# A decode step on one core: where three PV blocks stand among a softmax's steps, which engine takes a root, and how a mean is summed

## The chip, the cores and the metric

The kernel runs on one core of a Trainium2 chip. The metric is the device time of one execution in microseconds (us). Engines are called as the profile calls them: PE is TensorE's matmul and PEld its weight load, DVE is VectorE, ACT is ScalarE, POOL is GpSimd, and SP is SyncE, which here only issues transfers. All engines run their own instruction lists in order and wait for each other through semaphores.

## The reference

One token for each of 8 sequences goes through an attention block and a two-layer MLP block, each behind a layer norm. Only the last 2048 of the 8192 cached positions count.

```python
def _A_ref(x, k_cache, v_cache, wq, wo):          # x is layernormed: [8, 1, 512]
    # Hq = 32 query heads, Hkv = 8 cached heads, Dh = 128, W = 2048
    q = heads(x @ wq)
    k = jnp.repeat(k_cache[:, :, Sk - W:, :], 4, axis=1)
    v = jnp.repeat(v_cache[:, :, Sk - W:, :], 4, axis=1)
    p = _softmax(jnp.einsum("bhqd,bhkd->bhqk", q, k) * (Dh ** -0.5))
    o = jnp.einsum("bhqk,bhkd->bhqd", p, v)
    return o.reshape(B, Sq, Hq * Dh) @ wo

def _B_ref(x, w1, w2, w3, w4):                    # x is layernormed again
    ...                                           # the branch through w1, w2 shifts tokens
    x1 = x + hs                                   # with one token, hs is zero
    return x1 + _gelu(_layernorm(x1) @ w3) @ w4

h  = x + _A_ref(_layernorm(x), ...)
h2 = h + _B_ref(_layernorm(h), ...)               # the output, [8, 1, 512]
```

The second half needs two inverse roots of the variance of h. `r2` scales the first MLP product; `r1` scales the normed h that is added to the output.

## The kernel before, in words

**Items.** The work is cut into 64 items, one for each row (sequence) b and cached head g, numbered i = 8 b + g. An item has a K tile and a V tile of 2048 x 128. K is loaded four items at a time, V one at a time, all from SP's queue in the order in which the program issues them. V has 12 buffers: the load of V for item i waits until PE has used item i - 12 (`load_v`, L407).

**One loop over p.** The whole attention is written out by `for p in range(NITEM + LV + 1)` (L456), and each engine's order is the order of this loop. In step p PE transposes K of item p (L274), ACT and DVE copy the halves out (`evict`, L282 and L284), and PE does the scores of item p - 2 (`pe_QK`, L296). When a row's eight items are scored, its softmax is spread over the following steps: the maximum on DVE in step base = 8 b + 9 (`softmax_1`, L305); in base + 1 the maximum is turned by PE (L309) and joined and negated on DVE (`Mrow` L311, `negrow` L315); in base + 2 PE turns it back (L319), DVE copies it (`negcol`, L322), and ACT does the exponential (L323); in base + 3 PE transposes P (L333), DVE copies it out (`pT_sb`, L337) and prepares the sums (`lsel`, L341); in base + 4 PE adds them (L345) and DVE takes the reciprocal (`rL`, L347).

**PV in blocks of four.** For rows 0 to 6 the product with V is done for four items at once (`pe_PV4`, L365): 16 matmuls (L372) into the PSUM tile `o_rows`; ACT copies the result as bf16 (L379), DVE subtracts to get the rest that bf16 lost (L380). Some steps later `pe_oT` (L383) transposes both parts with 8 matmuls (L390), back into `o_rows`, and DVE scales the outcome into `oT_all` (L397). There is one `o_rows`: the next block waits for this scale. The last three such blocks begin at items 44 (row 5), 48 and 52 (row 6). Before the change they are issued like all others: block n in step n + 19, its transpose in step n + 20.

**The last row** goes item by item, from step 72 on: `pe_PV` with V as the stationary operand (L356), then its scale, and one step later its part of the output product. The first four heads go by `pe_wo_row` (L422), which also waits for the scale of block 52; the result is split in two bf16 parts (L429, L430), `pe_h0` adds them and x, and the other heads go by `pe_wo` (L449) into `hT_ps`, which then holds h transposed: 4 blocks of 128 features, 8 columns (sequences) each.

**The tail.** DVE copies h out (`hs`, L525), PE multiplies it with a matrix of ones to sum over the partitions (L527), DVE adds the four blocks (`msum`, L528) and subtracts the mean (`uT` L529 in bf16, `hc` L531). PE starts on w3 (L545), does the same sum for the squares in between (L550), and DVE reduces them to `vsum` (L554). POOL computes `r2` = (vsum + eps^2) to the power -0.5 in two instructions (L557, L558). DVE multiplies the product by it (`g_x`, L567, two halves), ACT applies Gelu (L569, two halves), and PE multiplies by w4 in three pieces as they land (L582). POOL goes on with `r1` (L570, L571), DVE makes `xb` (L572) and `fin` (L573) of it, adds the product (`fT`, L587), PE transposes it (L590), DVE copies it (L591), and SP stores it (L594).

Of the kernel before, what the change touches and what calls it, by code (L numbers as in the profile page):

```python
# [6 lines left out]
dt = mybir.dt  # L7
ACT = mybir.ActivationFunctionType
ALU = mybir.AluOpType
AX = mybir.AxisListType  # L10

B = 8
# [3 lines left out]
G = 8  # L16
# [8 lines left out]
EPS = 1e-5  # L25

NK = 3
KQ = 4
NV = 12
NKT = 4  # L30
LQK = 2
LV = 16
# [35 lines left out]
def bass_sequential_preLN__sliding_block_cached__mixer_s_mlp__decode_kernel(  # L68
# [19 lines left out]
    NITEM = NB * G  # L88
# [3 lines left out]
    with es:  # L92
        sb = lambda shape, dtype, name: es.enter_context(nc.sbuf_tensor(name, shape, dtype))
# [8 lines left out]
        ones_f = sb([128, 128], dt.float32, "ones_f")  # L102
# [7 lines left out]
        w4_sb = sb([128, FC, D], dt.bfloat16, "w4_sb")  # L110
        half = sb([128, B], dt.float32, "half")
        scratch = sb([128, 2], dt.float32, "scratch")

        x_sb = sb([B, D], dt.bfloat16, "x_sb")
        xln_b = sb([B, D], dt.bfloat16, "xln_b")
# [25 lines left out]
        orow = sb([128, 2, 512], dt.bfloat16, "orow")  # L141

        NH = KC * B
        hs = sb([128, NH], dt.float32, "hs")
        hc = sb([128, NH], dt.float32, "hc")
        hsq = sb([128, NH], dt.float32, "hsq")
        msum = sb([128, B], dt.float32, "msum")
        vsum = sb([128, B], dt.float32, "vsum")
        r1 = sb([128, B], dt.float32, "r1")
        r2 = sb([128, B], dt.float32, "r2")  # L150
        xb = sb([128, NH], dt.float32, "xb")
# [11 lines left out]
        sm = ps_t([128, 512], dt.float32, "sm")  # L163
# [4 lines left out]
        o_rows = ps_t([128, 512], dt.float32, "o_rows")  # L168
# [6 lines left out]
        PE, AC, DV, PO, SP = (Engine(S(n)) for n in ("s_pe", "s_act", "s_dve", "s_pool", "s_sp"))  # L175
# [7 lines left out]
        dma(AC, x_sb[:], A_x.rearrange("b s d -> (b s) d"), sem_x)  # L183
        X = (sem_x, 16)
        PO.op(lambda e: e.memset(half[:], -0.5))
        e_scr = PO.op(lambda e: e.memset(scratch[:], 1.0))
        e_xz = PO.op(lambda e: e.memset(xlnT[:], 0.0))
        e_iota = PO.op(lambda e: e.iota(iota_f[:], [[1, 128]], base=0, channel_multiplier=-1,
# [7 lines left out]
        e = DV.op(lambda e: e.bn_stats(st6[:, :], x_sb[:, :]), X)  # L196
        e = DV.op(lambda e: e.bn_aggr(mv[:, :], st6[:, :]), e)
        e = PO.op(lambda e: e.tensor_scalar(rstd[:, :], mv[:, 1:2], EPS, None, ALU.add), e)
        e = PO.op(lambda e: e.tensor_tensor(rstd[:, :], rstd[:, :], half[0:B, 0:1], ALU.pow), e)
# [7 lines left out]
        e = DV.op(lambda e: e.tensor_reduce(hsq[:, :], ident_f[:, :].rearrange("p (u h) -> p h u", u=4), AX.X, ALU.add))  # L207
# [9 lines left out]
        e = PE.op(pe_xT, e_xln, e_idb)  # L217
# [7 lines left out]
        for j in range(2):  # L225
# [9 lines left out]
            if j == 0:  # L235
                e = AC.op(lambda e: e.activation(qrow[:, 0, :], S_ps[0][:, :], ACT.Copy, scale=inv_sqrt_dh), e_q)  # L236
# [128 lines left out]
        def pe_PV4(i):  # L365
            b, g = divmod(i, G)
            v0 = i % NV

            def f(e):
                for c in range(NC):  # L370
                    u = c % 4
                    ins = e.matmul(o_rows[32 * u:32 * (u + 1), :], pT_sb[:, b % 2, c, :],  # L372
                                   vnat[:, v0:v0 + KQ, c * DH:(c + 1) * DH], start=(c < 4), stop=(c >= NC - 4),
                                   tile_position=(0, 32 * u), skip_group_check=True)
                return ins
            e_pv = PE.op(f, V(i), V(i + 1), V(i + 2), V(i + 3), e_pT[b], e_sc4.get(i - KQ))
            for k in range(KQ):
                e_PV[i + k] = e_pv
            e = AC.op(lambda e: e.activation(orow[:, 0, :], o_rows[:, :], ACT.Copy), e_pv, e_oT.get(i - KQ))  # L379
            e_olo[i] = DV.op(lambda e: e.tensor_tensor(orow[:, 1, :], o_rows[:, :], orow[:, 0, :], ALU.subtract), e)  # L380


        def pe_oT(i):  # L383
            b, g = divmod(i, G)

            def f(e):
                for t in range(KQ):
                    for part in range(2):
                        h = hq(g + t)
                        ins = e.matmul(o_rows[:, R * t:R * (t + 1)], orow[:, part, t * DH:(t + 1) * DH],  # L390
                                       sel32[:, h:h + R], start=(part == 0), stop=(part == 1), skip_group_check=True)
                return ins
            e_oT[i] = PE.op(f, e_olo[i], e_selb)
            e_scale[b] = e_sc4[i] = scale(b, slice(R * g, R * (g + KQ)), o_rows[:, 0:R * KQ], e_oT[i])

        def scale(b, heads, src, *waits):
            return DV.op(lambda e: e.tensor_tensor(oT_all[:, heads, b], src, rL[:, b % 2, heads], ALU.mult),  # L397
                         e_rL[b], e_oz, *waits)
# [13 lines left out]
        hT_ps = S_ps[0]  # L412
# [39 lines left out]
            e_wo.append(PE.op(f, e_sc7[g]))  # L452

        LAST = NB - 1
        E_LAST = G * LAST + G - 1 + LQK
        for p in range(NITEM + LV + 1):  # L456
            if p < NITEM:
                if p % KQ == 0:
                    load_k(p)
                if p == 1:  # L460
                    e_qblk = q_turn()
                pe_T(p)
                evict(p)
            if p in WO_AT:
                n = WO_AT.index(p)
                hh = H // len(WO_AT)
                dma(SP, wo_v[:, n * hh:(n + 1) * hh, :],
                    A_wo[n * hh * DH:(n + 1) * hh * DH, :].rearrange("(h p) n -> p h n", p=DH), sem_wo, e_q)
            for b in range(NB):
                base = G * b + (G - 1) + LQK  # L470
                if p == base + 1:
                    softmax_2(b)
                elif p == base + 2:
                    softmax_3(b)
                elif p == base + 3:
                    softmax_4(b)
                elif p == base + 4:
                    softmax_5(b)
            if 0 <= p - LQK < NITEM:
                pe_QK(p - LQK)  # L480
                b, g = divmod(p - LQK, G)
                if g == G - 1:
                    softmax_1(b)
            i = p - LV
            if 0 <= i < NITEM:
                load_v(i)
                b, g = divmod(i, G)
                heads = slice(R * g, R * (g + 1))
                if b < LAST:
                    if i % KQ == 0 and i:  # L490
                        pe_oT(i - KQ)
                    elif i % KQ == KQ - 1:
                        pe_PV4(i - KQ + 1)
                else:
                    if g == 0:
                        pe_oT(i - KQ)
                    dst = kbank[g % 3][:, 0:R]
                    pe_PV(i, dst, e_lo[NITEM - 1], e_hi[NITEM - 1], e_lo[NITEM - 2], e_hi[NITEM - 2],
                          e_sc7.get(g - 3))
                    e_sc7[g] = scale(b, heads, dst, e_PV[i])  # L500
            g = i - 1 - G * LAST
            if g == NR:
                pe_h0()
            if 0 <= g < NR:
                pe_wo_row(g)
            elif g >= NR:
                pe_wo(g)
# [9 lines left out]
        v3 = lambda t: t.rearrange("p (n b) -> p n b", b=B)  # L517
        vr = lambda t: t.rearrange("p (n b) -> p b n", b=B)

        def bc(t):  # L520
            a = t[:, :]
            return bass.AP(tensor=a.tensor, offset=a.offset, ap=[a.ap[0], [0, KC], [1, B]])


        e_hs = DV.op(lambda e: e.tensor_copy(hs[:, :], hT_ps[:, 0:NH]), e_wo[-1])  # L525
        st1, st2 = sm[:, 0:NH], o_rows[:, 0:NH]
        e = PE.op(lambda e: e.matmul(st1, ones_f[:, :], hs[:, :], start=True, stop=True), e_hs, e_rL[LAST])  # L527
        e_ms = DV.op(lambda e: e.tensor_reduce(msum[:, :], vr(st1), AX.X, ALU.add), e)  # L528
        e_u = DV.op(lambda e: e.scalar_tensor_tensor(v3(uT[:, :]), bc(msum), -1.0 / D, v3(hs[:, :]),  # L529
                                                     ALU.mult, ALU.add), e_ms)  # L530
        e_hc = DV.op(lambda e: e.scalar_tensor_tensor(v3(hc[:, :]), bc(msum), -1.0 / D, v3(hs[:, :]),  # L531
                                                      ALU.mult, ALU.add))
        e_sq = DV.op(lambda e: e.scalar_tensor_tensor(hsq[:, :], hc[:, :], (1.0 + EPS) / D, hc[:, :], ALU.mult, ALU.mult),
# [20 lines left out]
        e_vs = DV.op(lambda e: e.tensor_reduce(vsum[:, :], vr(st2), AX.X, ALU.add), e_st2)  # L554


        e = PO.op(lambda e: e.tensor_scalar(r2[:, :], vsum[:, :], EPS * EPS, None, ALU.add), e_vs)  # L557
        e_r2 = PO.op(lambda e: e.tensor_tensor(r2[:, :], r2[:, :], half[:, :], ALU.pow), e)  # L558

        def bcf(t):  # L560
            a = t[:, :]
# [3 lines left out]
        for n in range(2):  # L565
# [1 line left out]
            e = DV.op(lambda e, n=n, cs=cs: e.tensor_tensor(v3(g_x[:, cs]), v3(y_ps[n][:, 0:FH * B]), bcf(r2),  # L567
                                                            ALU.mult), e_y[n], e_r2)
            e_gT.append(AC.op(lambda e, cs=cs: e.activation(gT[:, cs], g_x[:, cs], ACT.Gelu_apprx_tanh), e))  # L569
        e = PO.op(lambda e: e.tensor_scalar(r1[:, :], vsum[:, :], EPS * (1.0 + EPS), None, ALU.add))  # L570
        e = PO.op(lambda e: e.tensor_tensor(r1[:, :], r1[:, :], half[:, :], ALU.pow), e)  # L571
        e = DV.op(lambda e: e.tensor_tensor(v3(xb[:, :]), v3(hc[:, :]), bc(r1), ALU.mult), e)  # L572
        e_fin = DV.op(lambda e: e.scalar_tensor_tensor(fin[:, :], xb[:, :], math.sqrt(1.0 + EPS), hs[:, :],  # L573
                                                       ALU.mult, ALU.add), e)

# [56 lines left out]
```

## Time and profile before

| | us |
|---|---|
| median of 3 runs (lowest, highest) | 201.53 (200.86, 202.16) |
| the profiled execution, its own time | 201.4 |
| its span | 199.2 |
| busy in that span: PE, PEld | 151.7, 99.7 |
| busy: ACT, DVE, POOL | 88.0, 83.1, 9.6 |
| transfers, from HBM | 79.18 MB, 398 GB/s over the span |

The span runs from the first to the last instruction of the profiled execution; the execution's time has 2.2 us more around it. All times in the lines below count from the start of the span. Transfers fill the 16 DMA engines for 96.8% of the span, but a share over the whole span hides that the last 6 us have none: what happens after the last K tile's landing is to be read from the chain of waits and the timeline of that stretch.

### The profile page before, as it was taken

To read this page: it belongs to the slowest core of one execution; us is meant where nothing else is said; L and a number is where in the kernel's file an instruction comes from. 1 tells how busy PE (TensorE), PEld (TensorE's weight loads), DVE (VectorE), ACT (ScalarE), POOL (GpSimd) and SP (SyncE) were. 2 spreads that over 40 slices of the span, in tenths; PEclk is the share of its full clock that TensorE was granted. 3 is DMA by queue.
4 is the path that set the end of the run, shared out by engine and by line. 5 is a ranking of instruction groups with operands and counts; after the bars stand their busy time and mean duration, and the time that the engine had idled before them with its cause. 6 is when DMAs were issued, how large, how long until landed. Compare 5 with 4: busy or idle time off the path is not lost.

```text
span 199.2 us, 4634 instructions
## 1 busy us (share of the span) xinstructions
PE 151.7 (76%) x2077; PEld 99.7 (50%) x2077; DVE 83.1 (42%) x181; ACT 88.0 (44%) x101; POOL 9.6 (5%) x17
## 2 busy tenths in 40 slices
PE   0037999999972999369982999398959798759753
PEld 0014666666641756157641756175727473226753
DVE  7403646446531446214541446234644354242221
ACT  2003766866741485324841485347544754310300
POOL 8300000000000000000000000000000000000043
PEclk9999999999997699967996699969996999655555
DMA  6999999999999999999999999999999999999950
GB/s 232 454 415 428 421 428 404 419 429 417 402 432 410 438 407 410 428 421 425 398 441 401 447 401 444 403 436 412 443 402 443 406 420 415 420 415 415 397 176 2
DMA packets 18275, 79.48 MB, mean 399 GB/s; under 512 B 1480, under 2 KB 7376, under 8 KB 16080
## 3 DMA queue, kind: packets, MB, share of 16 engines
q1 hardware_dynamic: 18240, 79.18, 96.8%
q8 instruction: 16, 0.26, 0.5%
q10 hardware_dynamic: 16, 0.01, 0.0%
q14 instruction: 3, 0.02, 0.0%
HBM read 79.18 MB, written 0.01 MB: 398 GB/s over the span
## 4 chain that ended last, share of the span: by engine, by line
DMA 60%; PE 28%; SPq 3%; DVE 3%; ACT 1%; POOL 1%; POOLq 1%; issue 1%; DVEq 0%
DMA knat<-in_A_k_cache_dram 51%; PE kT_ps L274 13%; DMA vnat<-in_A_v_cache_dram 10%; PE S_ps L296 6%; SPq L179 3%; PE o_rows L372 2%; PE kT_ps L356 2%; PE kT_ps L422 1%; DVE orow L380 1%; PE o_rows L390 1%; ACT orow L379 1%; PE S_ps L449 1%; POOLq L598 1%; POOL r L558 1%; PE sm L345 1%
## 5 line engine op out<-in xcount | busy, mean ns | idle before, releaser
L282 ACT ACTIVATE kT_sb<-kT_ps 128x1024 bf16<-128x1024 bf16 x64 | 65.4, 1024 | 61.4 <-PE kT_ps L274 61.4
L274 PE MATMUL kT_ps<-ident_b,knat 128*128 128x128 bf16 x1024 | 75.7, 233 | 20.5 <-DMA knat<-in_A_k_cache_dram 20.5
L274 PEld LDWEIGHTS kT_ps<-ident_b,knat 128*128 128x128 bf16 x1024 | 64.4, 105 | 45.1 <-DMA knat<-in_A_k_cache_dram 26.8
L284 DVE COPY kT_sb<-kT_ps 128x1024 bf16<-128x1024 bf16 x64 | 44.4, 694 | 59.3 <-PE kT_ps L274 59.3
L296 PE MATMUL S_ps<-kT_sb,qblk 128*32 128x512 bf16 x256 | 41.2, 612 | 0.0
L380 DVE TENSOR_TENSOR orow<-o_rows,orow 128x512 bf16<-128x512 f32 x14 | 9.7, 691 | 27.2 <-ACT orow L379 27.2
L372 PE MATMUL o_rows<-vnat,pT_sb 128*32 128x512 bf16 x224 | 16.5, 417 | 2.6 <-DMA vnat<-in_A_v_cache_dram 2.6
L379 ACT ACTIVATE orow<-o_rows 128x512 bf16<-128x512 f32 x14 | 8.6, 614 | 12.3 <-PE o_rows L372 12.3
L323 ACT ACTIVATE P_sb<-S_ps,negcol 128x512 bf16<-128x512 f32 x8 | 11.3, 1410 | 5.8 <-DVE negcol L322 5.8
L372 PEld LDWEIGHTS o_rows<-vnat,pT_sb 128*32 128x32 bf16 x224 | 6.3, 103 | 10.4 <-issue 7.9
L296 PEld LDWEIGHTS S_ps<-kT_sb,qblk 128*32 128x32 bf16 x256 | 7.3, 94 | 5.5 <-issue 1.6
L557 POOL TENSOR_SCALAR r<-vsum 128x8 f32<-128x8 f32 x1 | 0.2, 238 | 184.5 <-DVE vsum L554 184.5
L390 PEld LDWEIGHTS o_rows<-sel,orow 128*128 128x128 bf16 x112 | 3.9, 101 | 10.1 <-DVE orow L380 7.0
L390 PE MATMUL o_rows<-sel,orow 128*128 128x4 bf16 x112 | 5.1, 167 | 3.3 <-DVE orow L380 3.3
L230 PE MATMUL S_ps<-wbig,xlnT 128*32 128x512 bf16 x32 | 3.6, 630 | 5.1 <-DMA wbig<-in_A_wq_dram 5.1
L213 PE MATMUL sm<-ident_b,xln_b 8*128 8x8 bf16 x4 | 0.3, 174 | 7.7 <-DVE xln_b L201 7.7
L236 ACT ACTIVATE qrow<-S_ps 128x512 bf16<-128x512 f32 x1 | 0.6, 597 | 12.2 <-PE S_ps L230 12.2
L305 DVE TENSOR_REDUCE mcol<-S_ps 128x1 f32<-128x512 f32 x8 | 5.5, 682 | 0.3 <-PE S_ps L296 0.3
L356 PEld LDWEIGHTS kT_ps<-pT_sb,vnat 128*128 128x128 bf16 x128 | 4.0, 104 | 1.8 <-issue 1.8
L230 PEld LDWEIGHTS S_ps<-wbig,xlnT 128*32 128x32 bf16 x32 | 1.3, 139 | 6.6 <-issue 6.6
L356 PE MATMUL kT_ps<-pT_sb,vnat 128*128 128x4 bf16 x128 | 4.5, 167 | 0.0
L238 DVE TENSOR_SCALAR qrow<-S_ps 128x512 bf16<-128x512 f32 x1 | 0.7, 692 | 8.3 <-PE S_ps L230 8.3
(81 smaller groups left out, 87.0 us busy)
## 6 DMA issues: line engine op xcount, KB each, us to landing
knat<-in_A_k_cache_dram SPq DMA_DIRECT2D x16, 2048.0 KB, 19.4
vnat<-in_A_v_cache_dram SPq DMA_DIRECT2D x64, 512.0 KB, 18.6
wbig<-in_A_wq_dram SPq DMA_DIRECT2D x1, 4096.0 KB, 12.2
wbig<-in_A_wo_dram SPq DMA_DIRECT2D x4, 1024.0 KB, 20.3
w_sb<-in_B_w_dram SPq DMA_DIRECT2D x1, 1792.0 KB, 13.1
w_sb<-in_B_w_dram SPq DMA_DIRECT2D x1, 896.0 KB, 15.0
w_sb<-in_B_w_dram SPq DMA_DIRECT2D x1, 768.0 KB, 16.4
w_sb<-in_B_w_dram SPq DMA_DIRECT2D x1, 128.0 KB, 9.6
```

Source lines behind the costliest of these rows:

```text
L179: e.dma_start(dst, src).then_inc(sem, 16)
L274: ins = e.matmul(kT_ps[i % 2][:, n * 128:(n + 1) * 128], knat[:, i // KQ % NK, r * DH:(r + 1) * DH], ident_b[:, :], is_transpose=True)
L282: e_lo[i] = AC.op(lambda e: e.activation(kT_sb[:, i % NKT, 0:W // 2], kT_ps[i % 2][:, 0:W // 2], ACT.Copy), e_Tlo[i], e_QK.get(i - NKT))
L284: e_hi[i] = DV.op(lambda e: e.tensor_copy(kT_sb[:, i % NKT, W // 2:W], kT_ps[i % 2][:, W // 2:W]), e_Thi[i], e_QK.get(i - NKT))
L296: ins = e.matmul(S_ps[b % 2][32 * t:32 * (t + 1), :], qblk[:, b, g - g % KQ + t, at:at + H], kT_sb[:, i % NKT, :].rearrange("p (n t) -> p ...
L305: e_max[b] = DV.op(lambda e: e.tensor_reduce(mcol[:, :], S_ps[b % 2][:, :], AX.X, ALU.max), e_QK[G * b + G - 1], e_mT.get(b - 1))
L323: e_exp[b] = AC.op(lambda e: e.activation(P_sb[:, j, :].rearrange("p (c a w) -> p c w a", c=4, w=KQ), S_ps[j][:, :].rearrange("p (c w a) - ...
L356: ins = e.matmul(dst, vnat[:, i % NV, c * DH:(c + 1) * DH], pT_sb[:, b % 2, c, hq(g):hq(g) + R], start=(c == 0), stop=(c == NC - 1))
L372: ins = e.matmul(o_rows[32 * u:32 * (u + 1), :], pT_sb[:, b % 2, c, :], vnat[:, v0:v0 + KQ, c * DH:(c + 1) * DH], start=(c < 4), stop=(c > ...
L379: e = AC.op(lambda e: e.activation(orow[:, 0, :], o_rows[:, :], ACT.Copy), e_pv, e_oT.get(i - KQ))
L380: e_olo[i] = DV.op(lambda e: e.tensor_tensor(orow[:, 1, :], o_rows[:, :], orow[:, 0, :], ALU.subtract), e)
L390: ins = e.matmul(o_rows[:, R * t:R * (t + 1)], orow[:, part, t * DH:(t + 1) * DH], sel32[:, h:h + R], start=(part == 0), stop=(part == 1), ...
```

## The change

There are three edits. First, the steps in which the last blocks of four are issued come from a table `AT`, with three entries for each block: the step of its matmuls, that of its copy and subtraction (now a function of their own, `o_parts`), and that of its transpose. Every block keeps its old steps but the three that begin at items 44, 48 and 52: they take 65, 65 and 67; 67, 68 and 69; and 71, 71 and 73. Step 65 is the one in which the last scores are made and the last row's maximum is taken; the softmax's further steps are 66 to 69. Second, `r2` is made by a Sqrt on ACT and a reciprocal on DVE; POOL makes only `r1`, and now waits for `vsum` itself. Third, the four blocks of h are added first (`hsum`, DVE), and the ones-matmul is done on that sum, with 8 columns in place of 32; `uT` and `hc` read the mean from PSUM, and `hs` is copied behind `hsum`.

```diff
+        eps2 = sb([128, 1], dt.float32, "eps2")
+        s2 = sb([128, B], dt.float32, "s2")
...
+        PO.op(lambda e: e.memset(eps2[:], EPS * EPS))
...
             for k in range(KQ):
                 e_PV[i + k] = e_pv
-            e = AC.op(lambda e: e.activation(orow[:, 0, :], o_rows[:, :], ACT.Copy), e_pv, e_oT.get(i - KQ))
+
+        def o_parts(i):
+            e = AC.op(lambda e: e.activation(orow[:, 0, :], o_rows[:, :], ACT.Copy), e_PV[i], e_oT.get(i - KQ))
             e_olo[i] = DV.op(lambda e: e.tensor_tensor(orow[:, 1, :], o_rows[:, :], orow[:, 0, :], ALU.subtract), e)
...
+        AT = {i: (i + KQ - 1 + LV, i + KQ - 1 + LV, i + KQ + LV) for i in range(0, G * LAST, KQ)}
+        n = G * LAST
+        AT[n - 12] = NITEM - 1 + LQK, NITEM - 1 + LQK, NITEM + LQK + 1
+        AT[n - 8] = NITEM + LQK + 1, NITEM + LQK + 2, NITEM + LQK + 3
+        AT[n - 4] = n - 1 + LV, n - 1 + LV, n + 1 + LV
...
-                if b < LAST:
-                    if i % KQ == 0 and i:
-                        pe_oT(i - KQ)
-                    elif i % KQ == KQ - 1:
-                        pe_PV4(i - KQ + 1)
-                else:
-                    if g == 0:
-                        pe_oT(i - KQ)
+                if b == LAST:
                     dst = kbank[g % 3][:, 0:R]
                     pe_PV(i, dst, e_lo[NITEM - 1], e_hi[NITEM - 1], e_lo[NITEM - 2], e_hi[NITEM - 2],
                           e_sc7.get(g - 3))
                     e_sc7[g] = scale(b, heads, dst, e_PV[i])
+            for n, at in AT.items():
+                if at[2] == p:
+                    pe_oT(n)
+            for n, at in AT.items():
+                if at[0] == p:
+                    pe_PV4(n)
+                if at[1] == p:
+                    o_parts(n)
...
-        e_hs = DV.op(lambda e: e.tensor_copy(hs[:, :], hT_ps[:, 0:NH]), e_wo[-1])
-        st1, st2 = sm[:, 0:NH], o_rows[:, 0:NH]
-        e = PE.op(lambda e: e.matmul(st1, ones_f[:, :], hs[:, :], start=True, stop=True), e_hs, e_rL[LAST])
-        e_ms = DV.op(lambda e: e.tensor_reduce(msum[:, :], vr(st1), AX.X, ALU.add), e)
+        e = DV.op(lambda e: e.tensor_reduce(hsum[:, :], vr(hT_ps[:, 0:NH]), AX.X, ALU.add), e_wo[-1])
+        e_hs = DV.op(lambda e: e.tensor_copy(hs[:, :], hT_ps[:, 0:NH]))
+        msum, st2 = sm[:, 0:B], o_rows[:, 0:NH]
+        e_ms = PE.op(lambda e: e.matmul(msum, ones_f[:, :], hsum[:, :], start=True, stop=True), e, e_rL[LAST])
...
-        e = PO.op(lambda e: e.tensor_scalar(r2[:, :], vsum[:, :], EPS * EPS, None, ALU.add), e_vs)
-        e_r2 = PO.op(lambda e: e.tensor_tensor(r2[:, :], r2[:, :], half[:, :], ALU.pow), e)
+        e = AC.op(lambda e: e.activation(s2[:, :], vsum[:, :], ACT.Sqrt, bias=eps2[:, :], scale=1.0), e_vs)
+        e_r2 = DV.op(lambda e: e.reciprocal(r2[:, :], s2[:, :]), e)
...
-        e = PO.op(lambda e: e.tensor_scalar(r1[:, :], vsum[:, :], EPS * (1.0 + EPS), None, ALU.add))
+        e = PO.op(lambda e: e.tensor_scalar(r1[:, :], vsum[:, :], EPS * (1.0 + EPS), None, ALU.add), e_vs)
```

More of the change, by code (lines that the diff above doesn't have):

```diff
@@ L146, in bass_sequential_preLN__sliding_block_cached__mixer_s_mlp__decode_kernel @@
         hsq = sb([128, NH], dt.float32, "hsq")
-        msum = sb([128, B], dt.float32, "msum")
+        hsum = sb([128, B], dt.float32, "hsum")
         vsum = sb([128, B], dt.float32, "vsum")
@@ L454, in bass_sequential_preLN__sliding_block_cached__mixer_s_mlp__decode_kernel @@
         LAST = NB - 1
-        E_LAST = G * LAST + G - 1 + LQK
+        AT = {i: (i + KQ - 1 + LV, i + KQ - 1 + LV, i + KQ + LV) for i in range(0, G * LAST, KQ)}
[3 more added lines that the diff above has]
+        AT[n - 4] = n - 1 + LV, n - 1 + LV, n + 1 + LV
         for p in range(NITEM + LV + 1):
@@ L518, in bass_sequential_preLN__sliding_block_cached__mixer_s_mlp__decode_kernel, with bc @@
         vr = lambda t: t.rearrange("p (n b) -> p b n", b=B)
-        def bc(t):
-            a = t[:, :]
+        def bc(a):
             return bass.AP(tensor=a.tensor, offset=a.offset, ap=[a.ap[0], [0, KC], [1, B]])
-        e_hs = DV.op(lambda e: e.tensor_copy(hs[:, :], hT_ps[:, 0:NH]), e_wo[-1])
-        st1, st2 = sm[:, 0:NH], o_rows[:, 0:NH]
-        e = PE.op(lambda e: e.matmul(st1, ones_f[:, :], hs[:, :], start=True, stop=True), e_hs, e_rL[LAST])
-        e_ms = DV.op(lambda e: e.tensor_reduce(msum[:, :], vr(st1), AX.X, ALU.add), e)
+        e = DV.op(lambda e: e.tensor_reduce(hsum[:, :], vr(hT_ps[:, 0:NH]), AX.X, ALU.add), e_wo[-1])
+        e_hs = DV.op(lambda e: e.tensor_copy(hs[:, :], hT_ps[:, 0:NH]))
+        msum, st2 = sm[:, 0:B], o_rows[:, 0:NH]
+        e_ms = PE.op(lambda e: e.matmul(msum, ones_f[:, :], hsum[:, :], start=True, stop=True), e, e_rL[LAST])
         e_u = DV.op(lambda e: e.scalar_tensor_tensor(v3(uT[:, :]), bc(msum), -1.0 / D, v3(hs[:, :]),
-                                                     ALU.mult, ALU.add), e_ms)
+                                                     ALU.mult, ALU.add), e_ms, e_hs)
         e_hc = DV.op(lambda e: e.scalar_tensor_tensor(v3(hc[:, :]), bc(msum), -1.0 / D, v3(hs[:, :]),
@@ L569, in bass_sequential_preLN__sliding_block_cached__mixer_s_mlp__decode_kernel @@
             e_gT.append(AC.op(lambda e, cs=cs: e.activation(gT[:, cs], g_x[:, cs], ACT.Gelu_apprx_tanh), e))
-        e = PO.op(lambda e: e.tensor_scalar(r1[:, :], vsum[:, :], EPS * (1.0 + EPS), None, ALU.add))
+        e = PO.op(lambda e: e.tensor_scalar(r1[:, :], vsum[:, :], EPS * (1.0 + EPS), None, ALU.add), e_vs)
         e = PO.op(lambda e: e.tensor_tensor(r1[:, :], r1[:, :], half[:, :], ALU.pow), e)
-        e = DV.op(lambda e: e.tensor_tensor(v3(xb[:, :]), v3(hc[:, :]), bc(r1), ALU.mult), e)
+        e = DV.op(lambda e: e.tensor_tensor(v3(xb[:, :]), v3(hc[:, :]), bc(r1[:, :]), ALU.mult), e)
         e_fin = DV.op(lambda e: e.scalar_tensor_tensor(fin[:, :], xb[:, :], math.sqrt(1.0 + EPS), hs[:, :],
```

## The prediction, made before the changed kernel ran

> **What bounds the kernel now.** I read the page first, then the chain of waits from 165 us to the end, then the timeline of the same stretch, then the landing times of the last transfers.
>
> ```profile
> span 199.2 us, 4634 instructions
> PEclk9999999999997699967996699969996999655555
> DMA  6999999999999999999999999999999999999950
> ```
>
> One slice is 4.98 us. The transfers run without a gap until about 190 us, and the granted TensorE clock is 0.5 from about 171 us to the end (the table by windows has 1.00 at 170 to 171 and 0.53 at 171 to 172). The last K tile lands at 159.45. From there on the chain no longer contains a transfer: the end is set by instructions that wait for one another. These are the pieces that the change touches, from the chain of waits (start, duration, what):
>
> ```profile
> 165.83 0.55 PE S_ps L296 x3
> 166.38 0.90 PE o_rows L372 x13
> ...
> 167.93 0.70 DVE orow L380
> ...
> 168.68 0.35 PE o_rows L390 x8
> 169.03 0.58 PE S_ps L296 x4
> ...
> 171.38 0.58 PE sm L319 x2
> 171.96 1.86 PE o_rows L372 x16
> ...
> 176.33 1.86 PE o_rows L372 x16
> ...
> 179.59 0.37 PE o_rows L390 x8
> 179.97 0.85 PE kT_ps L356 x32
> 180.82 0.55 PE kT_ps L422 x4
> ```
>
> Three times PE finishes a PV block (L372) and then waits for ACT's copy (0.61) and DVE's subtraction (0.70) before it may transpose back (L390); the first time, the last QK (169.03) and with it the whole last softmax stand behind that wait. At the end, the timeline:
>
> ```profile
> 185.23 1.28 ACT L569 ACT_TABLE_LOAD   x1
> 191.66 0.19 DVE L554 TENSOR_REDUCE vsum<-o_rows 128x8 f32<-128x32 f32 x1 [0.83 <-PE o_rows L550]
> 192.26 1.67 POOL L558 TENSOR_TENSOR r<-r,half 128x8 f32<-128x8 f32 x1
> 194.28 0.39 ACT L569 ACTIVATE gT<-g_x 128x56 bf16<-128x56 f32 x2 [7.77 <-DVE g_x L567]
> 196.27 0.19 DVE L573 SCALAR_TENSOR_TENSOR fin<-xb,hs 128x32 f32<-128x32 f32 x1
> ```
>
> The power on POOL alone holds everything for 1.67; a table load on ACT costs 1.28 and here runs early, right behind the copy at L429, not behind the wait of its Gelu.
>
> **Part 1, the blocks at items 44, 48 and 52.** Nothing is removed: the same 3 x (16 + 8) matmuls, copies, subtractions and scales are issued in another order. I lay them out again from 166.38 with the rows' own durations and hops (0.02 to 0.05).
>
> QK(62) follows QK(61) directly, 166.38 to 166.93; QK(63) needs DVE's eviction, done at 165.87 + 0.69 = 166.56, so 166.93 to 167.50. The maximum (0.69) ends at 168.22. PE meanwhile does block 44, 167.48 to 168.38, then L309 to 168.58. ACT's copy ends at 169.01, the subtraction at 169.73. This is the new wait: on DVE, Mrow is queued behind that subtraction, idle from 168.22. Mrow 0.29 and negrow 0.23 end at 170.27; L319 (0.38 at full clock, 0.58 at half) ends by 170.7 to 170.9; the exponential starts at 170.90 to 171.1 against 172.19. Block 48 must wait for block 44's transpose (0.35) and scale (0.23): it starts at about 171.35 against 171.96, **0.61 earlier**, and ends at 173.21 at half clock. Then P's transpose to 173.72, pT 0.41, lsel 0.2, subtraction of 48 to 175.02, its transpose to 175.42, its scale to 175.67: block 52 starts at 175.72 against 176.33, the same 0.61. So the shadow of the exponential gives no second gain here.
>
> Block 52 ends at 177.58. PE now does PV(56) and PV(57) (0.85 together) during the copy and the subtraction, transposes at 178.98 to 179.35, the scale ends at 179.60, and L422 starts at 179.65 against 180.82. **Part 1: 1.17.**
>
> Other queues: on SP the loads of V 56 to 59 wait for block 44, those of V 60 to 63 for block 48, and w3 and w4 are queued behind them. The first group is issued at 168.4 rather than 167.30, the second at 173.2 rather than 173.84. V 56 took 8.3 us from issue to landing, while 512 KB at the 419 GB/s of that stretch needs 1.25, so several us of work are queued ahead of it and I cost the 1.1 at nothing. V 55, issued by 160.2 and landing 14.2 to 14.5 later, is there by 174.7; block 52 wants it at 175.72. V 63 lands at about 184.4, PV(63) starts at 186.5.
>
> **Part 2, the mean.** Before: copy (0.20), ones-matmul (0.65), reduction (0.20), uT. After: reduction, ones-matmul, uT, with the copy under the matmul. The first two cost the same (L528 0.192, L525 0.191). The reduction behind the matmul goes with its hop, 190.06 to 190.31: **0.25**. The matmul has 8 columns in place of 32: between 0.58 (L319, one column) and 0.64 (L527); I take no gain. uT reads the mean from PSUM: L567, which also does, takes 0.210 for 56 columns, so at most 0.02 more; none.
>
> **Part 3, the root.** From the end of vsum (191.86) to the first Gelu took 2.42. Now: hop 0.02, Sqrt, then the table load, then Gelu. Sqrt isn't in the trace. Below, L192 takes 0.20 for one column; above, 0.20 + (1.41 - 0.60) = 1.01, from L323, whose pointer bias and accumulation over 512 columns make it 0.81 dearer than L236. It is nearest to L569 (0.24 for 56 columns): 0.25. The load is 1.28 and, as at 1.34 us and 185.23, the next instruction follows in 0.02. Sum 0.02 + 0.25 + 0.02 + 1.28 + 0.02 = 1.59: **0.83 saved**. The load for Sqrt itself can go where Gelu's went, at about 184. Under Gelu's load run the reciprocal (between 0.15, L322, and 0.35, L347 with four times the columns; 0.18) and g_x (0.20), 0.44 with hops, against 1.30: a cover of 0.86.
>
> The Trainium skill, "ScalarE: Activation LUTs", section "What ACT_TABLE_LOAD costs", speaks against this: each switch is a load of about 1283 ns and a drain of about 1380 ns. The two loads of this trace show 1.28 and no pause behind; by the page's figure this part would lose 0.55 instead, and the time would be 200.5.
>
> **Part 4, the other root.** POOL does r1 straight after vsum: 0.24 + 1.67 end 1.5 us before the last w4 matmul, and xb and fin are long done. Before, fT started 0.25 after that matmul's end (196.31 to 196.56), now 0.05: **0.20**. The added memset on POOL (0.10) sits in the first us, where PE waits for wq until 13.08: nothing; without that cover 0.03 to 0.1.
>
> **The sum.** 1.17 + 0.25 + 0.83 + 0.20 = 2.45. The profiled execution took 201.4 (span 199.2 and 2.2 around it): 201.4 - 2.45 = 198.95. The median of the runs is 0.13 above that execution, so **199.1**.
>
> **What is late next** are the transfers. w3 lands at 175.63 + 13.1 = 188.7, wanted at 190.56 - 1.42 = 189.1. The second piece of w4 lands at 176.65 + 16.4 = 193.05; the first half of w4's matmuls now ends at 194.68 - 2.25 + 0.79 = 193.2. There are 0.2 to 0.4 us of slack, so more than about 0.2 beyond the forecast can't be had while the stream stays as it is.
>
> **Rivals.** (a) *The reciprocal waits for POOL's power.* POOL now starts r1 at the moment when DVE wants the reciprocal. The trace has DVE held by POOL:
>
> ```profile
> 6.52 0.94 POOL L200 MEMSET oT_all<- 128x1024 bf16 x1
> 6.60 1.01 DVE L201 TENSOR_SCALAR xln_b<-x_sb,mv,rstd 8x512 bf16<-8x512 bf16 x1 [1.00 <-POOL rstd L199]
> ```
>
> 512 columns on 8 partitions take 1.01, ending just behind the memset. Against it: L567 ran beside POOL's L570 in its usual 0.2. If held, the reciprocal starts when the power ends, 2.07 after vsum (0.08 + 0.25 + 0.07 + 1.67), and Gelu at 2.07 + 0.02 + 0.18 + 0.02 + 0.20 + 0.02 = 2.51 in place of 1.59: 0.92 lost, **200.0**. The Trainium skill, "SBUF — State Buffer", section "Who interferes with whom", says that a DVE copy, cast or tensor_scalar that uses both ports and a GpSimd instruction exclude each other entirely; the reciprocal isn't on its list. If it belongs there, the sum is this rival's.
>
> (b) *The table switch is dearer*: Gelu's load goes only when g_x is done (1.59 + 0.42 = 2.01, **199.5**), and Sqrt's load also behind its wait (1.28 more, **200.8**). Against it: 185.23. Sqrt at its upper bound gives 199.9.
>
> (c) *The moved blocks bring nothing*: if the clock falls to 0.5 at 167.5 rather than 171, block 44 takes 1.86 instead of 0.90 and L309 0.2 more, which with DVE's order eats Part 1: **200.3**. For it: slices at 0.6 and 0.7 elsewhere; against it: PE is denser here than before. If the clock falls later, block 48 shrinks by up to 0.96, but w4 then holds the end at 198.9.
>
> (d) *Slower: a gap in the stream.* Block 44's delay on SP's queue becomes idle transfer time and moves w3 and w4. If all of the 1.1 turns into a gap, w4's second piece lands at 194.15 and the time is 200.0. It is slower than before once that piece lands after 196.31 - 0.79 = 195.5, a gap of 2.5; a gap of 4.6 gives **203.6**. Against it: the 8.3 us of landing.
>
> **Chances.** Forecast 0.62 (its own range 198.5 to 199.7), (a) 0.14, (b) 0.08, (c) 0.08, (d) 0.08. 1% of 201.53 is 2.0, about what a measurement of this kernel tells from no change: the line lies at 199.5. Four fifths of the forecast, 0.50, and 0.02 of (b) fall below it; slower than 203.5 is (d), 0.08; the rest, 0.40, is within 1%. The range 198.3 to 200.9 takes in the forecast with (a), (b) and (c) and leaves out (d) and some tails.
>
> **What would show it.** Right: both last QKs back to back before block 44; block 48 about 0.6 and L422 about 1.2 earlier; no L528; on ACT one table load near 184 and one of 1.28 directly behind Sqrt, Gelu 1.6 after vsum; fT directly behind the last w4 matmul. Wrong: a reciprocal that ends with POOL's power (a), ACT idle before a load (b), block 44 at 1.9 us (c), or PE waiting for w_sb (d).

## The result, and the profile after

| | before | after |
|---|---|---|
| median of 4 runs each on one chip (lowest, highest), us | 201.39 (200.86, 202.16) | 198.68 (198.55, 198.94) |
| ratio of the times, 95% interval | | 0.9864 (0.9828 to 0.9901) |
| the profiled execution: time, span, difference | 201.4, 199.2, 2.2 | 198.55, 196.8, 1.75 |
| the same kernel once more, 6 runs: median (lowest, highest), ratio | | 198.68 (198.33, 199.00), 0.9852 (0.9823 to 0.9880) |

The forecast was 199.1, in a range of 198.3 to 200.9. The kernel is faster by 1.4%. The predicted span, 199.2 - 2.45 = 196.75, is met to 0.05; the remaining 0.4 lies outside the span. From the page of the kernel after, the span, the two rows by slices and the first line on the chain:

```profile
span 196.8 us, 4638 instructions
PEclk9999999999999699966999699969997999965555
DMA  6999999999999999999999999999999999999991
DMA 70%; PE 22%; SPq 5%; DVE 1%; issue 1%; ACT 0%
```

One slice is now 4.92 us. Two things differ from before: the half clock begins a slice later, and the transfers, which used to end 6 us before the span did, now reach into its last slice. They end no later (the last piece lands at 193.4 before and at 193.5 now); the span is shorter. The chain of waits of the same execution (start, duration, what) shows the consequence:

```profile
165.90 1.49 PE S_ps L299 x11
167.39 0.90 PE o_rows L375 x15
...
171.20 1.05 PE o_rows L375 x16
...
176.29 16.84 DMA w_sb<-in_B_w_dram
...
193.18 0.93 PE S_ps L593 x28
```

Both last QKs are done before block 44 (L299, then L375), as laid out in the forecast. Block 48 starts at 171.20, 0.76 earlier than before. But the chain no longer goes through the tail's arithmetic: it passes from block 48 to the last weights, and ends on the second piece of w4, which lands at 176.29 + 16.84 = 193.13. The windows of this execution say why (us, then for PE, PEld, DVE, ACT, POOL the busy time and count, the granted clock, the DMA share, GB/s):

```profile
173.00:174.00 1.00, 0.56 (x7) 0.44 (x8) 1.00 (x4) 0.00 (x0) 0.00 (x0) 0.77 1.01 414
```

The granted clock is the last column but two. Its mean of 0.77 is full speed for 0.54 of that microsecond and half speed for the rest, so the clock fell at about 173.5, not at 171 as in the profile before. So block 48 took 1.05 instead of about 1.9, everything behind it came 0.98 earlier than forecast, and PE then waited for transfers. The timeline of the tail (start, duration, engine and line, in brackets the idle time before and what ended it):

```profile
178.67 0.62 PE L427 MATMUL kT_ps<-wbig,oT_all 128*32 128x512 bf16 x4 [0.32 <-DVE oT_all L402]
...
183.15 1.28 ACT L568 ACT_TABLE_LOAD   x1
...
188.89 0.57 PE L556 MATMUL kT_ps<-uT,w_sb 128*128 128x8 bf16 x16 [0.96 <-DMA w_sb<-in_B_w_dram]
...
190.19 0.30 ACT L568 ACTIVATE s<-vsum,eps 128x8 f32<-128x8 f32 x1 [5.76 <-DVE vsum L565]
...
190.51 1.28 ACT L580 ACT_TABLE_LOAD   x1
...
190.58 1.68 POOL L582 TENSOR_TENSOR r<-r,half 128x8 f32<-128x8 f32 x1
...
191.81 0.39 ACT L580 ACTIVATE gT<-g_x 128x56 bf16<-128x56 f32 x2
192.20 1.89 PE L593 MATMUL S_ps<-gT,w_sb 128*128 128x8 bf16 x56 [1.22 <-ACT gT L580]
...
194.12 0.22 DVE L598 TENSOR_TENSOR fT<-fin,S_ps 128x32 bf16<-128x32 f32 x1 [1.42 <-PE S_ps L593]
```

L427 (before: L422) starts 2.15 earlier than the 180.82 of before. uT is done at 188.16 and PE could start on w3 about 0.05 later, at 188.21; it starts at 188.89, released by the landing of w3: 0.68 of waiting. On ACT the load for Sqrt stands at 183.15, far ahead of Sqrt; the load for Gelu follows Sqrt in 0.02; Gelu follows it in 0.02.

### The profile page after: what moved, and what is told of

It reads as the page before. It is cut to its first block, busy times and chain, and to the rows that moved or that the text cites. A ratio compares the mean times of both kernels' runs of the same rounds, so it can differ in the third digit from the quotient of the medians.

```text
span 196.8 us, 4638 instructions
## 1 busy us (share of the span) xinstructions
PE 149.0 (76%) x2077; PEld 98.1 (50%) x2077; DVE 83.1 (42%) x182; ACT 89.6 (46%) x103; POOL 7.7 (4%) x16
## 4 chain that ended last, share of the span: by engine, by line
DMA 70%; PE 22%; SPq 5%; DVE 1%; issue 1%; ACT 0%
DMA knat<-in_A_k_cache_dram 52%; PE kT_ps L277 13%; DMA vnat<-in_A_v_cache_dram 10%; DMA w_sb<-in_B_w_dram 9%; PE S_ps L299 6%; SPq L181 5%; PE o_rows L375 1%; PE o_rows L395 1%; PE sm L336 1%; PE S_ps L593 0%; DVE orow L385 0%; ACT orow L384 0%; PE o_rows L250 0%; PE sm L322 0%; PE sm L348 0%
## 5 line engine op out<-in xcount | busy, mean ns | idle before, releaser
L277 PE MATMUL kT_ps<-ident_b,knat 128*128 128x128 bf16 x1024 | 74.3, 231 | 21.8 <-DMA knat<-in_A_k_cache_dram 21.8
L277 PEld LDWEIGHTS kT_ps<-ident_b,knat 128*128 128x128 bf16 x1024 | 63.2, 104 | 46.2 <-DMA knat<-in_A_k_cache_dram 28.0
L299 PE MATMUL S_ps<-kT_sb,qblk 128*32 128x512 bf16 x256 | 40.9, 612 | 0.0
L375 PE MATMUL o_rows<-vnat,pT_sb 128*32 128x512 bf16 x224 | 15.6, 399 | 3.7 <-DMA vnat<-in_A_v_cache_dram 2.9
L375 PEld LDWEIGHTS o_rows<-vnat,pT_sb 128*32 128x32 bf16 x224 | 6.2, 101 | 11.1 <-issue 8.3
L299 PEld LDWEIGHTS S_ps<-kT_sb,qblk 128*32 128x32 bf16 x256 | 7.2, 93 | 6.0 <-issue 1.2
L322 PE MATMUL sm<-ones_f,negrow 1*128 1x1 f32 x16 | 3.0, 256 | 1.5 <-DVE negrow L318 1.5
```

Of the source, the lines that this page charges most:

```text
L277: ins = e.matmul(kT_ps[i % 2][:, n * 128:(n + 1) * 128], knat[:, i // KQ % NK, r * DH:(r + 1) * DH], ident_b[:, :], is_transpose=True)
L299: ins = e.matmul(S_ps[b % 2][32 * t:32 * (t + 1), :], qblk[:, b, g - g % KQ + t, at:at + H], kT_sb[:, i % NKT, :].rearrange("p (n t) -> p ...
```

## The experiments

Times are medians; each ratio is against runs of the kernel before on the same chip, whose medians in the three sets were 201.34, 201.50 and 201.23. "Outside the span" is a run's time less its span. Two theories stand against each other: the parts of the sum bring what the forecast gave each (about 1.17 by the blocks, 0.25 by the mean, 1.03 by the root together with the freed fT), or one part brought nearly everything and another nothing. A second question came from the profile after: does the change now stop at the transfers?

### The blocks alone (e1_blocks_only)

The edit, on the kernel before, is the loop part of the change, with neither the mean nor the root:

```diff
+        AT[n - 12] = NITEM - 1 + LQK, NITEM - 1 + LQK, NITEM + LQK + 1
+        AT[n - 8] = NITEM + LQK + 1, NITEM + LQK + 2, NITEM + LQK + 3
+        AT[n - 4] = n - 1 + LV, n - 1 + LV, n + 1 + LV
```

> The kernel before with the first edit alone (the blocks at items 44, 48 and 52 moved; root and mean as before). Theory: the moved blocks are worth 1.2 to 2.15 us at L422 by the clock that PE happens to have at 171 to 173 us, but w3 lands at about 188.8 whatever PE does, so its first matmul can't be more than 1.75 us earlier than before (190.56), and the root on POOL then runs as before: 1.2 to 1.75 us less than the kernel before, about 199.8. Rival (the parts simply add, transfers bind nowhere): 2.15 less where the clock stays full to 173.5, about 199.2, with no wait of PE for w_sb in the profile.

Measured: 200.03, ratio 0.9926 (0.9901 to 0.9952); median span 198.2 against 199.2, so 1.0 in the span, and 0.3 outside it. That is below the 1.2 to 1.75 that were expected. In its profile the clock fell at about 171.9, and the line that was L422 starts at 179.05, 1.77 earlier; w3's matmuls start at 189.01, 1.55 earlier. They begin 0.20 behind uT's end (188.81), elsewhere 0.05: w3, issued at 174.28, landed 14.6 later, at 188.9, so its landing already holds PE by 0.15 here. The part is real; its size hangs on when the clock falls.

### The root alone, and the mean alone (e2_root_only, e3_mean_only)

Both kernels are the one after without the three lines below; in e2 the mean, in e3 the root is as before. They keep the loop in its new form with its standard rule, and that rule by itself puts PV(56) ahead of block 52's transpose, which the kernel before did the other way round. The expectations didn't count this.

```diff
-        AT[n - 12] = NITEM - 1 + LQK, NITEM - 1 + LQK, NITEM + LQK + 1
-        AT[n - 8] = NITEM + LQK + 1, NITEM + LQK + 2, NITEM + LQK + 3
-        AT[n - 4] = n - 1 + LV, n - 1 + LV, n + 1 + LV
```

> The kernel before with the second edit alone (Sqrt on ACT, reciprocal on DVE, r1 alone on POOL). Theory: vsum to the first Gelu takes 1.65 us instead of 2.42 (0.77) and fT no longer waits for fin (0.20); no transfer is late, since w4's second piece lands at 193.1 and is wanted at 194.1: 0.97 less, about 200.4. Rival (the table switch costs as much as the power it replaces once it is on the path): no change, 201.4.

> The kernel before with the third edit alone (the blocks of h added before the ones-matmul). Theory: one reduction with its hop less, 0.25 to 0.30, about 201.1; from h's last matmul to uT's end 1.09 instead of 1.36. Rival: the copy behind the reduction or the mean read from PSUM eats it: 201.4.

Measured: the root 199.46, ratio 0.9904 (0.9874 to 0.9934), span 197.65; the mean 200.49, 0.9953 (0.9931 to 0.9976), span 198.65. The root's time is 0.9 below what was expected: a miss, of which the order (0.43, next) and the time outside the span (0.38, at the end of this part) make up 0.8. The chain of waits of the root's kernel shows its own two steps:

```profile
191.22 0.02 issue
...
193.25 1.65 PE S_ps L591 x56
194.90 0.02 issue
194.92 0.23 DVE fT L596
```

From vsum's end (191.22) to w4's first matmul it is 2.03, against 2.82 before (191.86 to 194.68), and from there to fT 1.67, against 1.88 before (194.68 to 196.56): 0.79 and 0.21, together 1.00. The expectation had 0.97, the forecast 0.83 + 0.20 = 1.03 for Parts 3 and 4. The chain of waits of the mean's kernel shows its own step clearly:

```profile
188.47 0.61 PE sm L533 x2
...
189.35 0.59 PE kT_ps L550 x16
```

From the end of h's last matmul (188.20) to the start of w3's it is 1.15, against 1.42 before (189.14 to 190.56): 0.27, where 0.25 was forecast. The runs of this kernel lie in two groups of spans (197.9 to 198.4 and 198.9 to 199.6), too far apart to show 0.27: against the order alone (next, median span 198.7) its median span of 198.65 would give the mean only 0.05.

### The order alone (e9_order_only)

To settle what e2 and e3 had carried along: the kernel before with the loop in its new form and no block moved, so that nothing but that order differs. The transpose, ahead of the last row's PV so far, now stands behind it.

```diff
+        AT = {i: (i + KQ - 1 + LV, i + KQ - 1 + LV, i + KQ + LV) for i in range(0, G * LAST, KQ)}
...
-                    if g == 0:
-                        pe_oT(i - KQ)
                     dst = kbank[g % 3][:, 0:R]
...
                     e_sc7[g] = scale(b, heads, dst, e_PV[i])
+            for n, at in AT.items():
+                if at[2] == p:
+                    pe_oT(n)
...
```

> The kernel before with one thing of the first edit: in step 72 PV(56) is issued ahead of block 52's transpose instead of behind it (the kernels with the root alone and the mean alone have this too). Theory: PE does PV(56) while it would wait for the subtraction of block 52, so L422 starts 0.43 earlier and the span falls by 0.43, to about 198.8. Rival (PV(56) only takes the place of the wait and the next thing then waits for the scale): no change.

Measured: 200.88, ratio 0.9969 (0.9947 to 0.9990); span 198.7 against 199.3. Its chain of waits:

```profile
180.41 0.37 PE o_rows L392 x8
180.78 0.43 PE kT_ps L356 x16
181.21 0.55 PE kT_ps L424 x4
```

From the transpose to L424 it is 0.80, against 1.23 before (179.59 to 180.82): 0.43, as expected, since one PV with its 16 matmuls now stands between the two in place of two. The change issues two PVs ahead of the transpose: there it is 0.70 in both profiles (177.97 to 178.67, and 178.90 to 179.60 in the repeat below), 0.53 less than before, where the forecast's second half of Part 1 was 1.17 - 0.61 = 0.56. By median spans the order brings 0.6 and the root, against it, 198.7 - 197.65 = 1.05, but the spans of the two kernels scatter over 1.8 and 1.5; the steps in the chains are the better measure. By them the first theory holds.

### Less to wait for (e4_less_w3)

```diff
-        dma(SP, w3_sb[:, :, :], B_w3.rearrange("(k p) f -> p k f", p=128), sem_w3)
+        dma(SP, w3_sb[:, 0:KC - 1, :], B_w3.rearrange("(k p) f -> p k f", p=128)[:, 0:KC - 1, :], sem_w3)
...
-                        ins = e.matmul(..., w3_sb[:, kc, fc * 128:(fc + 1) * 128],
+                        ins = e.matmul(..., w3_sb[:, kc % (KC - 1), fc * 128:(fc + 1) * 128],
```

> The changed kernel, but a quarter of w3 (448 KB) isn't loaded; the matmuls that would use that quarter use the first quarter again, so the values differ and the instructions are the same. Theory (the transfers hold the end of the changed kernel): all landings behind it come 1.1 us earlier, PE's wait for w3 (0.68) and for w4's second piece (0.17) go, and the time falls by 0.8 to 0.9 to about 197.8. Rival (the end is set by the instructions, the waits for transfers only fill time that another wait would fill): no change, 198.7.

Measured: 198.21, ratio 0.9836 (0.9806 to 0.9866); span 196.4 against the changed kernel's 196.8. No wait for a transfer is left in its tail: from L427 (179.37) to fT (193.93) it takes 14.56, where the profiled execution of the change took 15.45, with 0.68 and 0.17 of waiting. But the clock of this execution fell at about 172.3, and uT was done at 188.86; by then w3 had landed in the first profile too (188.8). So its profile doesn't test the 0.68. The times say more: four of the six (197.51 to 198.22) lie below the lowest of the ten of the changed kernel (198.33), so in some executions the transfers do hold that kernel's end. The median gains only 0.47, half of what was expected, with an interval that overlaps those of the change, and the times scatter over 1.5 (197.51 to 198.98), against 0.4 and 0.7 for the two sets of the changed kernel. A reading that fits: only executions in which the clock falls late have anything to gain here. It was put to the next run.

### The same kernel once more (a0_after_again)

The changed kernel, with no edit.

> The changed kernel once more, to stand on one chip beside the others. Theory (w3's and w4's landings hold its end): again 198.7, and little spread, since neither the clock's phase nor the compute stretch before reaches the end. Rival (the instructions hold it): the spread of 1.5 us that the kernel without a quarter of w3 showed.

Measured: 198.68, span 196.8, as the first time. The median and the small spread (0.67) came as expected. But in this profile the clock fell at about 170.8, as the forecast had assumed. First its window from 171 us (columns as above), then its chain of waits:

```profile
171.00:172.00 1.00, 0.91 (x12) 0.45 (x16) 0.00 (x0) 1.00 (x2) 0.00 (x0) 0.50 1.02 418
```

```profile
171.09 1.90 PE o_rows L375 x16
...
175.58 1.92 PE o_rows L375 x16
...
179.60 0.62 PE kT_ps L427 x4
...
189.14 0.59 PE kT_ps L556 x16
...
190.78 1.28 ACT L580
...
192.47 1.65 PE S_ps L593 x56
194.12 0.02 issue
194.14 0.24 DVE fT L598
```

Now no transfer stands on the chain, and the steps fall on the forecast's: L427 at 179.60 (forecast 179.65), w3's matmuls at 189.14 (189.1 was the forecast's time for wanting w3), w4's at 192.47 (192.43), fT at 194.14 (194.10). In the first profile fT starts at 194.12. So the arithmetic with an early fall of the clock and the transfers with a late one end at the same time, within 0.02 in these two profiles; in the four variants below fT starts at 194.07 to 194.26. The expectation's cause, the landings alone, is not what this profile shows.

### Cutting the last transfers finer, and more work moved forward (e7_finer, e11_pv_early, e10_pv_early_finer)

If transfers and arithmetic tie, neither change alone can bring anything, and both together might. e7 halves w3 by columns and cuts w4 into four pieces; e11 issues PV(62) and PV(63) directly behind PV(61); e10 does both.

```diff
-        dma(SP, w3_sb[:, :, :], B_w3.rearrange("(k p) f -> p k f", p=128), sem_w3)
+        w3_src = B_w3.rearrange("(k p) f -> p k f", p=128)
+        for n in range(2):
+            dma(SP, w3_sb[:, :, n * F // 2:(n + 1) * F // 2], w3_src[:, :, n * F // 2:(n + 1) * F // 2], sem_w3[n])
...
-        W4_AT = (0, 7, 13, FC)
+        W4_AT = (0, 7, 11, 13, FC)
...
-            if 0 <= i < NITEM:
+            for i in ({NITEM - 3: (NITEM - 3, NITEM - 2, NITEM - 1), NITEM - 2: (), NITEM - 1: ()}.get(i, (i,))):
+                if not 0 <= i < NITEM:
+                    continue
...
```

> The changed kernel with the last transfers cut finer: w3 in two halves by columns, w4 in pieces of 7, 4, 2 and 1 instead of 7, 6 and 1, the matmuls waiting for their own piece. Theory (landings hold the end): PE starts w3 at 188.2 instead of 188.9, and behind the last landing (193.1 to 193.4) only 1 to 3 of w4's 14 chunks are left instead of 7: 0.4 to 0.6 less, about 198.1. Rival (the instructions hold the end, or smaller pieces land later): 198.7 or more.

> The changed kernel with PV(62) and PV(63) issued straight behind PV(61), into PE's idle stretch before the split of the first four heads is ready (0.99 us in the profile of the changed kernel). This takes up to 0.86 us off the instructions' path and nothing off the transfers. Theory (in the changed kernel instructions and transfers end within some tenths of each other): only 0.1 to 0.3 less, about 198.5, with PE waiting for w3 and for w4's second piece in the profile. Rival (instructions alone hold the end): 0.8 less, 197.9.

> The same with the last transfers cut finer as well (w3 in two halves by columns, w4 in 7, 4, 2 and 1). Theory (both bounds tie, so only lowering both pays): about 0.6 less than the changed kernel, 198.0, though each alone gives little. Rival (transfers hold the end whatever their cut): 198.5 to 198.7.

Measured: e7 198.68, ratio 0.9855 (0.9828 to 0.9883); e11 198.77, 0.9878 (0.9849 to 0.9907); e10 198.63, 0.9878 (0.9843 to 0.9912). None is told apart from the change, and the gains that the theories gave (198.1 for e7, 198.5 for e11, 198.0 for e10) didn't come. e7 ended on the arithmetic (the clock fell at about 170.5, no wait for w_sb). e11 waited 0.57 for w3 (uT is done at 188.42, PE could start 0.05 later and starts at 189.04) and 0.16 for w4. e10 is the miss that teaches. Its clock fell at about 173.6, as late as in the first profile. Its first w4 matmul starts at 191.73, 0.47 ahead of the first profile and 0.74 ahead of the repeat; yet fT starts at 194.07, only 0.05 and 0.07 earlier. Its chain of waits, and its windows from 190 us:

```profile
183.66 9.72 DMA w_sb<-in_B_w_dram
...
193.43 0.62 PE S_ps L599 x12
```

```profile
190.00:191.00 1.00, 0.51 (x19) 0.42 (x16) 0.60 (x3) 0.98 (x2) 0.92 (x2) 0.50 0.84 295
191.00:192.00 1.00, 0.27 (x11) 0.30 (x12) 0.18 (x1) 0.71 (x3) 0.78 (x1) 0.50 0.54 193
192.00:193.00 1.00, 0.93 (x35) 0.84 (x32) 0.20 (x2) 0.00 (x0) 0.00 (x0) 0.50 0.51 174
```

A piece of 256 KB, issued at 183.66, lands at 193.38. The stream of this execution runs at 385 GB/s from 189 to 190 us, and then at 295, 193 and 174 GB/s, so all the last pieces land in this tail, however they are cut. Earlier arithmetic has no use as long as 79 MB take to about 193.4. Nor did the two moved PVs bring anything in this execution. The timeline of e10 has PV(63):

```profile
184.43 0.59 PE L360 MATMUL kT_ps<-pT_sb,vnat 128*128 128x4 bf16 x16 [0.66 <-DMA vnat<-in_A_v_cache_dram]
```

Issued early, it waits 0.66 for its own V, and everything behind it on PE waits too: uT is done at 188.34, against 188.16 in the first profile. So e10's lead at w4 comes from the first half of w3, for which PE doesn't wait, and not from the two PVs. In e11, whose clock fell at about 171.5, PV(63) waits 0.28; there the move gains 0.55 between L427 and uT (179.48 to 188.42, against 178.67 to 188.16), of the 0.86 that were expected at most.

### Does POOL's power hold DVE? (e6_probe)

The changed kernel with a second reciprocal and a copy of the same 128 x 8 values on DVE, while the power runs. Nothing reads them.

```diff
         e_r2 = DV.op(lambda e: e.reciprocal(r2[:, :], s2[:, :]), e)
+        DV.op(lambda e: e.reciprocal(probe[:, 0:B], s2[:, :]))
+        DV.op(lambda e: e.tensor_copy(probe[:, B:2 * B], s2[:, :]))
```

> The changed kernel with two more DVE instructions between the reciprocal and g_x, on the same 8 columns: a second reciprocal and a copy, both from SBUF to SBUF, into an unused tile. They fall into the 1.68 us in which POOL's power for r1 runs. Theory of the prediction's rival (a) (POOL's running instruction holds DVE out of SBUF's shared port): the copy, or both, last until the power ends, over 1 us, and g_x and Gelu start 1 us late. Other theory (POOL's power does not hold DVE): both take 0.15 to 0.25, and Gelu still starts behind its table load.

One execution took 198.69. Its timeline:

```profile
190.73 1.68 POOL L585 TENSOR_TENSOR r<-r,half 128x8 f32<-128x8 f32 x1
190.80 0.15 DVE L571 RECIPROCAL probe<-s 128x8 f32<-128x8 f32 x1
190.87 0.12 DVE L572 COPY probe<-s 128x8 f32<-128x8 f32 x1
```

Both run in 0.15 and 0.12 inside the power's 1.68. Spans on POOL are rough, so this doesn't say what POOL did at 190.8; it does say that DVE wasn't held until 192.4.

### Where the 0.4 outside the span comes from (c0_before_again, n1_dve_plus_one)

Before had 2.11 to 2.23 outside its span in every run, all kernels with parts of the change but e9 had 1.74 to 1.93. Counted with its semaphore entries, DVE's list has 189 entries in the traces of before and of e9, and 190 to 194 in all the others. c0 is the kernel before, unchanged; n1 is the kernel before with one memset on DVE in its first microseconds that nothing reads.

```diff
+        spare = sb([128, 8], dt.float32, "spare")
...
         e = DV.op(lambda e: e.tensor_reduce(hsq[:, :], ident_f[:, :].rearrange("p (u h) -> p h u", u=4), AX.X, ALU.add))
+        DV.op(lambda e: e.memset(spare[:, :], 0.0))
```

> The kernel before, unchanged, under another name. In all runs so far an execution of before takes 2.12 to 2.21 us more than its span, and every altered kernel 1.75 to 1.88, whatever was altered. Theory 1 (it comes with the program of before): again 2.2 around the span, 201.4. Theory 2 (it comes with how the kernel before is run among the others): 1.8 around the span, 201.0; then 0.38 us of every comparison belong to no edit.

> The kernel before with one more instruction on DVE: a memset of an unused 8-column tile, in the first microseconds, where DVE has nothing that anyone waits for. All kernels so far whose DVE list has 189 entries in the trace (before, twice, and the one with PV(56) reordered) take 2.12 to 2.23 us more than their span; all with 190 or 192 take 1.74 to 1.91. Theory (the length of DVE's list decides, not the edits): 1.8 around the span, the span unchanged near 199.2, so about 201.0. Rival (one of the edits does it): 2.2 around the span, 201.4.

Measured: c0 201.46, ratio 0.9999 (0.9973 to 1.0025), 2.12 to 2.20 outside the span. n1 200.85, ratio 0.9979 (0.9956 to 1.0003), span 199.05 against 199.0, 1.76 to 1.86 outside. One instruction of no use took the 0.38 away, with the span where it was. It goes with the length of this list in all these runs, but equally with the count of all instructions in the profile (4634 for before and e9, 4635 and more for the others), which n1 changes too. The mechanism stays open, since no profile reaches outside the span.

## Why the prediction was right, by its own steps

Gains in us, from the starts in the profiles (before; the first profile after; the repeat whose clock fell as assumed):

| step | forecast | after | repeat |
|---|---|---|---|
| to L422 / L427 (Part 1) | 1.17 | 2.15 | 1.22 |
| from there to h's last matmul | 0 | -0.06 | -0.07 |
| h's last matmul to w3's first (Part 2) | 0.25 | 0.26 - 0.68 of waiting | 0.27 |
| w3's first to vsum's end | 0 | 0.03 | 0 |
| vsum's end to w4's first matmul (Part 3) | 0.83 | 0.78 | 0.79 |
| w4's first matmul to fT (Part 4) | 0.20 | -0.04, with 0.17 of waiting | 0.21 |
| sum, at fT | 2.45 | 2.44 | 2.42 |

The starts of before, from its timeline, that the table counts from and the prediction's lines don't show:

```profile
190.56 0.59 PE L545 MATMUL kT_ps<-uT,w_sb 128*128 128x8 bf16 x16 [0.51 <-DVE uT L529]
...
194.68 1.63 PE L582 MATMUL S_ps<-gT,w_sb 128*128 128x8 bf16 x56 [2.01 <-ACT gT L569]
...
196.56 0.23 DVE L587 TENSOR_TENSOR fT<-fin,S_ps 128x32 bf16<-128x32 f32 x1
```

The -0.06 and -0.07 are a matter of reading: before, the first matmul of L422 starts at 180.75 by the timeline, beside the last ones of L356, while the chain counts it from 180.82.

**Part 1** is right in mechanism and, for a clock that falls at 171, in size to 0.05. That is in part luck: in the repeat block 52 starts 0.75 earlier than before (176.33 to 175.58), where 0.61 was forecast, and what follows brings 0.47 for 0.56. The term hangs on the moment of the clock's fall: 170.5 to 173.6 over the profiles taken, 173.5 and 170.8 in two of the changed kernel, 171.1 and 173.2 in two of the kernel before, so the moved blocks don't set it. It was the forecast's assumption that the fall would come as in the one profile it had; rival (c) named the other case and its consequence.

**What is late next** is right. It had w3 landing at 188.7 (188.8 in the first profile), w4's second piece at 193.05 (193.13), and said that no more than about 0.2 beyond the forecast could be had. The first profile brings 0.98 more in Part 1 and returns it, 0.68 at w3, 0.17 at w4, the rest in hops; e10, 0.74 ahead of the repeat at w4, is 0.07 ahead at fT.

**Part 2** is right, 0.27 in two kernels for 0.25. **Part 3** is 0.04 short: Sqrt took 0.30 and not 0.25. The switch of tables cost its load of 1.28 and nothing behind. The Trainium skill, "ScalarE: Activation LUTs", section "What ACT_TABLE_LOAD costs", has about 1380 ns of drain on top at every switch; these runs don't agree: 0.02 from the load's end to Gelu. The other load, for Sqrt, is issued ahead of Sqrt's wait, at 183.15, and is hidden. **Part 4** shows in the repeat, 0.21, fT 0.02 behind the last matmul; in the first profile w4's landing takes its place.

**The sum against the time.** The forecast for the span was 196.75, measured 196.8. In the first profile that is no test of the sum, since Part 1 was 0.98 larger and the transfers took it back; the repeat, with the clock that was assumed, is one: 2.42 for 2.45. The time is 198.68 and not 199.1 because the 2.2 outside the span were taken as fixed, and are 1.75 to 1.9 with this kernel. So of the 2.7 gained by the medians about 2.35 are the change's and some 0.36 are not due to anything that it moves.

**The rivals.** (a) fails: the reciprocal took 0.20 beside the power, and e6 shows that a later one, and a copy, were not held either. On this the Trainium skill, "SBUF — State Buffer", section "Who interferes with whom", counts a DVE copy among the instructions that can exclude GpSimd's work, and be excluded by it, while they use both ports. The copy here took 0.12 beside the power, whereas in the profile before a tensor_scalar on DVE took 1.01, to just behind the end of a memset on POOL; which ports the copy used no profile shows. (b) fails, by the 0.02 ahead of the load at 190.51. (c) comes about in its second half, a later fall of the clock, with the result that it named (198.9 with 2.2 outside the span; that execution took 198.55 with 1.75). (d) fails: no gap in the stream, w3 is issued at 174.08 and lands at 188.8 (before: 175.63 and 188.7).

**Chances.** "Faster by over 1%" had 0.52. The first interval reaches just past 0.99 (0.9901), that of the repeat ends at 0.9880. Without the part outside the span the ratio would be close to (198.68 + 0.36) / 201.39 = 0.9883: still beyond 1% by the medians, but an interval as wide as the first one (0.0037 to each side) would reach past 0.99. The margin beyond 1% owes that much to a gain that the forecast didn't have: luck.

## What to carry to other kernels

When several short waits at the end of a kernel are taken away, work out for each what lands next and when it is wanted; here a tie between weights and arithmetic, 0.2 to 0.4 us apart in the forecast, decided that nothing beyond it could be had, and none of three variants got beyond it. Work that is moved forward can run into the landing of its own operand, as PV(63) did in e10. A step's price taken from one profile holds only for the clock that this profile had: if the fall lies near the step, give both prices. To take an edit apart, look at what the frame of the edit changes by itself, since nearly half of what e2 gained beyond its expectation was an order that came with the rewritten loop.

## What was not expected of the hardware

**Time outside the span** is not a constant of the chip: 2.11 to 2.23 with 189 entries in DVE's list (4634 instructions in the profile), 1.74 to 1.93 with 190 to 194 (4635 and more), among them one kernel whose only difference is a memset without use. Of the 2.7 that the medians show for the change, 0.36 is of this kind.

**The end of a stream** is slow: with 385 GB/s at 189 to 190 us, e10's transfers ran at half of that two microseconds later. It isn't the cutting: in the profile before, 360 GB/s from 189 to 190 us are followed by 259, 195 and 150. Nor did the cutting help: e10's last piece landed at 193.7, that of the change as it is at 193.5.

**The fall of the clock** to 0.5 moved between 170.5 and 173.6 us from execution to execution. With the transfers as a floor, the changed kernel seems to hide that, which is a reading of the spreads and not shown singly: its times spread over 0.7 (198.33 to 199.00), those of the kernel before, in the first set of 17 runs, over 1.7 (200.69 to 202.40), and e4's, with the floor lowered, over 1.5.
